# Second expert tile of an attention, expert and token-mix kernel: token list, turns and decode steps moved

## Chip, core and metric

The kernel runs on one core of a Trainium2 chip. The metric is the device time of one launch, in microseconds. Three runs of the kernel before gave 435.61, 435.96 and 431.9; the median is 435.61. One further execution was profiled.

## What is computed

Activations and expert weights are float32; the mix weights `w_theta`, `w_tok_r`, `w_tok_i` and `w_ch` come as float64 and are handed to the kernel as 64-bit words. The reference, cut to what matters:

```
attn:  B 2, H 8, S 768, D 64; each row sees its 31 neighbours and 24 block summaries
       (max of 32 keys, mean of 32 values), softmax, times values        -> x (2,768,512)
moe:   logits = x @ w_gate; a sigmoid gate may keep the expert of the token before it
       out[s] = p[e] * relu(x[s] @ w1[e]) @ w2[e]     8 experts, 512 -> 1024 -> 512
mix:   theta = x @ w_theta; zr, zi = x*cos(theta), x*sin(theta)
       y = w_tok_r @ zr + w_tok_i @ zi; u = x + y; out = u + relu(u @ w_ch)
```

## The kernel before

**Stages.** Attention runs to about 76 us of the profile. Then tokens are sorted by expert and run through expert tiles of 256 tokens: six full tiles (j = 0 to 5) and one half tile of 128 tokens, to about 248 us. The token mix takes the rest.

**A full tile.** Each tile uses one expert. Its weights come in eight pieces of 512 KB: `w1` in pieces q = 0 to 3, `w2` in q = 4 to 7. The loop variable n counts pieces over all tiles (n = 8j + q), and every piece has two half steps, so h = 2q + half runs from 0 to 15 in a tile. TensorE works on two float32r parts, high and low: three groups of matmuls take high by high, and high by low either way. `ff1` (half steps 0 to 7) makes the hidden layer, twelve 256-column matmuls a half step; `ff2` (8 to 15) adds six 512-column matmuls a half step into the output.

**What feeds it.** `load_piece` (SP's DMA queue) fills one of four `wraw` buffers, six pieces ahead where a buffer is free. `split_piece` makes the high part `whi` on ScalarE (L595) and the low part `wlo` on VectorE (L596), three pieces ahead of TensorE, into one of five buffers each; for the first three pieces GpSimd makes `wlo`. The hidden layer leaves PSUM as `hh` (ScalarE, L638) and `hl` (VectorE, L639), through three `psh` buffers. `gather` fetches the token rows of a tile by an indirect DMA of GpSimd's queue; `xpose` turns them on TensorE (256 columns of the model width a call) and splits them into `xh` (ScalarE, L618) and `xl` (VectorE, L619). The output leaves as `y` (ScalarE, L711) and `scatter` (GpSimd's queue).

**Token lists.** A generator `route0` makes the lists of tiles 0 and 1, `route1` the others, in small VectorE operations between small matmuls. Its yields "hop" mark where TensorE is needed. The last part of `route0` is a matmul into `psi` (L484), the index arithmetic (`index_pair`) and the updates of `rem` and `hib`. `HOPS` says in which half steps of tile 0 `route1` goes on: 2, 4, 6 and 9.

**Decoding.** The twelve mix weights needed first (four `t`, 512 columns; eight `w`, 768 columns) are loaded as 64-bit words and decoded between the half steps. One weight is four calls of `step(bg2)`, which this document names A to D:

```
A  ScalarE: dg and dl from the raw words (L772, L773)
B  VectorE: three bit operations on dg (L775 to L777)
C  ScalarE: high part from dg (L780)
D  VectorE: low part (L782); then the load of the weight after the next
```

The very first call only issues two loads. `dg` has one buffer, so A of the next weight comes after D. `DEC[j]` holds the half steps of tile j behind which a call stands.

**Order.** No planner moves anything: each engine takes its instructions strictly in the order in which the loop writes them. In a half step that is: loads, list work, split (first half only), matmuls with what empties PSUM, gather, scatter, turn, and last the decode call.

Of the kernel before, what the change touches and what calls it, by code (L numbers as in the profile page):

```python
# [88 lines left out]
def tile_attn_moe_mix(ctx: ExitStack, tc: tile.TileContext, qT, kT, vp, gw, w1, w2, wth, wtok, wch, cst, msk, out):  # L89
# [288 lines left out]
    def prob(b, m):  # L378
        L = lg[b][:, :, 0:8]
        ex = small([128, 6, 8], "ex")  # L380
        V.tensor_tensor(ex, L, m.unsqueeze(2).to_broadcast([128, 6, 8]), op=ALU.subtract)
        A.activation(ex, ex, AF.Exp)
        s = small([128, 6], "s")
        V.tensor_reduce(s, ex, axis=AX.X, op=ALU.add)
        V.tensor_scalar(s, s, 1.0e-9, None, op0=ALU.add)
        V.reciprocal(s, s)
        V.tensor_tensor(ex, ex, oh[b][:, 0:6, :], op=ALU.mult)
        se = small([128, 6], "se")
        V.tensor_reduce(se, ex, axis=AX.X, op=ALU.add)
        V.tensor_tensor(pe[:, 6 * b:6 * b + 6], se, s, op=ALU.mult)  # L390
# [208 lines left out]
    def gather(j):  # L599
        xgs[j] = []  # L600
        for r in range(1 if j == HT else 2):
            c = 2 * j + r if j < HT else NPX + 2 + j
            t = xg_p.tile([128, DM], F32, name="xg", tag="xg")
            G.indirect_dma_start(out=t, out_offset=None, in_=xd[0:S, :] if j < 2 else xd,  # L604
                                 in_offset=bass.IndirectOffsetOnAxis(ap=ixg[:, c:c + 1], axis=0))
            xgs[j].append(t)

    def xpose(j, c2):
        if c2 == 0:
            xts[j] = (xt_p.tile([128, 4, TS], F32R, name="xh", tag="xh"), xt_p.tile([128, 4, TS], F32R, name="xl", tag="xl"))  # L610
        xh, xl = xts[j]
        ps = psM.tile([128, 2, TS], F32, name="psx2", tag="m")
        for cc in range(2):
            for r in range(2):
                c = 2 * c2 + cc
                T.transpose(ps[:, cc, 128 * r:128 * r + 128], xgs[j][r][:, 128 * c:128 * c + 128], idn)
        s = slice(2 * c2, 2 * c2 + 2)
        A.copy(xh[:, s, :], ps)  # L618
        V.tensor_tensor(xl[:, s, :], ps, xh[:, s, :].bitcast(F32), op=ALU.subtract)  # L619

    def ff1(j, q, mm):
        hi, lo = spl[j, q]
        hw = hi.rearrange("p (c f) -> p c f", c=4)
        lw = lo.rearrange("p (c f) -> p c f", c=4)
        xh, xl = xts[j]
        if mm == 0:
            hs[j, q] = psH.tile([128, 2, TS], F32, name="psh", tag="h")
        ps = hs[j, q]
        fs = slice(128 * mm, 128 * mm + 128)
        n = 0  # L630
        for a, x in ((hw, xh), (hw, xl), (lw, xh)):
            for c in range(4):
                T.matmul(ps[:, mm, :], a[:, c, fs], x[:, c, :], start=n == 0, stop=n == 11)  # L633
                n += 1
        if mm == 1:
            hh = h_p.tile([128, 2, TS], F32R, name="hh", tag="hh")
            hl = h_p.tile([128, 2, TS], F32R, name="hl", tag="hl")
            A.activation(hh, ps, AF.Relu)  # L638
            V.scalar_tensor_tensor(hl, ps, 0.0, hh.bitcast(F32), op0=ALU.max, op1=ALU.subtract)  # L639
            hs[j, q] = (hh, hl)  # L640

    def xpose_half():
        xts[HT] = (xt_p.tile([128, 4, TS], F32R, name="xh", tag="xh"), xt_p.tile([128, 4, TS], F32R, name="xl", tag="xl"))
        xh, xl = [t[:, :, 0:128] for t in xts[HT]]
        ps = psM.tile([128, 4, 128], F32, name="psx4", tag="m")
        for c in range(4):
            T.transpose(ps[:, c, :], xgs[HT][0][:, 128 * c:128 * c + 128], idn)
        A.copy(xh, ps)
        V.tensor_tensor(xl, ps, xh.bitcast(F32), op=ALU.subtract)
# [42 lines left out]
    def ff2(j, q, r):  # L692
        hi, lo = spl[j, 4 + q]
        hw = hi.rearrange("p (c f) -> p c f", c=2)
        lw = lo.rearrange("p (c f) -> p c f", c=2)
        hh, hl = hs[j, q]
        if q == 0:
            yps[j, r] = psY.tile([128, DM], F32, name=f"psy{r}", tag=f"y{r}")
        ps = yps[j, r]
        ts_ = slice(128 * r, 128 * r + 128)  # L700
        n = 0
        for a, w in ((hh, hw), (hh, lw), (hl, hw)):
            for f in range(2):
                T.matmul(ps, a[:, f, ts_], w[:, f, :], start=q == 0 and n == 0, stop=q == 3 and n == 5)  # L704
                n += 1
        if q == 3:
            if j <= NL:
                y = ys_p.tile([128, DM], F32, name="y", tag="y")
            else:
                y = h_p.tile([128, 2, TS], F32R, name="hh", tag="hh").bitcast(F32).rearrange("p a b -> p (a b)")  # L710
            A.copy(y, ps)  # L711
            ysb[j, r] = y
# [36 lines left out]
    def scatter(j, r):  # L749
        c = 2 * j + r if j < HT else NPX + 2 + j  # L750
        G.indirect_dma_start(out=yd, out_offset=bass.IndirectOffsetOnAxis(ap=ixs[:, c:c + 1], axis=0),  # L751
                             in_=ysb[j, r], in_offset=None)
# [62 lines left out]
    def step(gen):  # L815
        return next(gen, "end")
# [90 lines left out]
    for k in range(NG + 8):  # L907
# [6 lines left out]
        if k < NG:  # L914
            n, g = units[k]
# [51 lines left out]
    def hop(gen):  # L967
        r = None
        while r not in ("hop", "end"):
            r = step(gen)  # L970
            if r == "experts":
                flags["ready"] = True
# [27 lines left out]
    def piece(fn, n):  # L1000
        if n < NPC:
            j, q = divmod(n, 8)
            fn(j if j <= NL else HT, q)
# [3 lines left out]
    items1 = [f"t{k}" for k in range(4)] + [f"w{i}{r}" for i in range(4) for r in range(2)]  # L1007
    bg2 = dec_run(items1, lambda: wk1)
    items2 = [f"w{i}{r}" for i in range(4, 6) for r in range(2)] + [f"c{k}" for k in range(4)]
    DEC = [(0, 12, 13, 14, 15)] + [(0, 2, 4, 6, 8, 9, 11, 12, 14)] * 5  # L1010
    nld = LD
    for n in range(8 * NL + 8):
        j, q = divmod(n, 8)
        for half in range(2):
            h = 2 * q + half
            while nld <= n + LD and (nld < 16 or flags["ready"]):
                piece(load_piece, nld)
                nld += 1
            if n == 0 and half == 1:
                while step(state["bg"]) != "end":  # L1020
                    pass
                gather(1)
            if j == 0 and h in HOPS or j == 1 and h == 2:
                hop(bg)
            if half == 0:
                if n < LSX:
                    piece(split_piece, n + LS)
                if n >= LSX - 1:
                    piece(split_piece, n + LS + 1)
            if q < 4:  # L1030
                ff1(j, q, half)
            else:
                ff2(j, q - 4, half)
            if h == (3 if j == 1 else 1) and j > 0:
                gather(j + 1 if j < NL else HT)
            if h == 3 and j > 0:
                scatter(j - 1, 1)
            if j == 1 and h in (7, 11):
                prob(h // 8, mmax[h // 8])
            if j > 0 and h in (10, 11):  # L1040
                if j < NL:
                    xpose(j + 1, half)
                elif half == 0:
                    xpose_half()
            elif j == 0 and h == 14:
                xpose(1, 0)
                xpose(1, 1)
            if h == 14:
                scatter(j, 0)
            if h in DEC[j]:  # L1050
                step(bg2)
    for q in range(8):
        n = 8 * NL + 8 + q
# [426 lines left out]
```

## Time and profile before

| what | value |
|---|---|
| median of three runs | 435.61 us |
| profiled execution, its own time | 431.91 us |
| its span | 430.1 us |
| TensorE matmul, weight load busy | 411.0 us (96%), 353.8 us (82%) |
| VectorE, ScalarE, GpSimd busy | 309.5 us (72%), 230.9 us (54%), 118.4 us (28%) |
| mean granted TensorE clock | 0.996 |
| weight pieces | 56 loads of 512 KB, median 4.9 us to landing |
| mix weights | 12 loads of 768 KB, median 6.8 us; 8 of 512 KB |

The span is from the first instruction's start to the last one's end; the profiled execution's own time is 1.81 us longer. A busy TensorE is not one at its peak, since matmuls are pipelined and their ends are modelled. Busy shares are averages over three stages with different limits.

### The profile page before, as it was taken

To read this page: it belongs to the slowest core of one execution; us is meant where nothing else is said; L and a number is where in the kernel's file an instruction comes from. 1 tells how busy PE (TensorE), PEld (TensorE's weight loads), DVE (VectorE), ACT (ScalarE), POOL (GpSimd) and SP (SyncE) were. 2 spreads that over 40 slices of the span, in tenths; PEclk is the share of its full clock that TensorE was granted. 3 is DMA by queue.
4 is the path that set the end of the run, shared out by engine and by line. 5 is a ranking of instruction groups with operands and counts; after the bars stand their busy time and mean duration, and the time that the engine had idled before them with its cause. 6 is when DMAs were issued, how large, how long until landed. Compare 5 with 4: busy or idle time off the path is not lost.

```text
span 430.1 us, 7952 instructions
## 1 busy us (share of the span) xinstructions
PE 411.0 (96%) x2917; PEld 353.8 (82%) x2917; DVE 309.5 (72%) x737; ACT 230.9 (54%) x424; POOL 118.4 (28%) x108
## 2 busy tenths in 40 slices
PE   8999998799899999999998899999999999999993
PEld 7677877688798989898987788888888788899883
DVE  7575668688897968987899578797988843622731
ACT  5873866645566757775678566564654421211300
POOL 8293732610122105040211121343334710100000
PEclk9999999999999999999999999999999999999998
DMA  8992984984787978989587362322300010100022
GB/s 289 409 391 79 255 263 148 339 307 139 262 269 238 337 244 271 334 261 328 191 299 243 128 231 83 104 74 84 112 26 8 28 40 24 50 13 27 12 75 80
DMA packets 45072, 76.31 MB, mean 177 GB/s; under 512 B 3424, under 2 KB 28256, under 8 KB 44256
## 3 DMA queue, kind: packets, MB, share of 16 engines
q1 hardware_dynamic: 42944, 68.89, 47.9%
q0 software_dynamic: 2080, 6.82, 4.2%
q8 instruction: 25, 0.41, 0.4%
q14 instruction: 23, 0.19, 0.1%
HBM read 62.85 MB, written 12.85 MB: 176 GB/s over the span
## 4 chain that ended last, share of the span: by engine, by line
PE 42%; ACT 3%; DVE 3%; DMA 1%; issue 1%; ACTq 0%
PE ya L1240 15%; PE yb L1240 8%; PE pth L1178 8%; PE psch L1265 8%; DVE wlo L596 1%; DMA wraw<-in_w_dram 1%; PE psxt L1115 1%; ACT whi L595 1%; PE psy L685 1%; PE pl L743 0%; ACT dg L772 0%; ACT dl L773 0%; DVE hl L639 0%; PE yb L1231 0%; DVE dg L776 0%
## 5 line engine op out<-in xcount | busy, mean ns | idle before, releaser
L596 DVE TENSOR_TENSOR wlo<-wraw,whi 128x1024 fp32r<-128x1024 f32 x53 | 64.4, 1219 | 14.0 <-ACT whi L595 14.0
L595 ACT CAST whi<-wraw 128x1024 fp32r<-128x1024 f32 x56 | 58.1, 1046 | 4.5 <-DMA wraw<-in_w_dram 3.3
L751 POOL DMA_INDIRECT yd<-y,ixs x13 | 17.0, 1307 | 118.9 <-ACT y L711 98.4
L250 ACT ACTIVATE neg<-neg,mn 128x120 f32<-128x120 f32 x96 | 30.2, 385 | 22.1 <-DVE mn L248 21.4
L633 PE MATMUL psh<-xl,whi 128*128 128x256 f32 x192 | 31.2, 284 | 2.0 <-DVE xl L619 1.9
L1208 POOL TENSOR_TENSOR r<-r,x 128x512 f32<-128x512 f32 x10 | 13.0, 1304 | 69.9 <-ACT r L1203 69.9
L633 PE MATMUL psh<-xh,whi 128*128 128x256 f32 x192 | 31.4, 285 | 0.6 <-DVE hl L639 0.6
L633 PE MATMUL psh<-xh,wlo 128*128 128x256 f32 x192 | 30.8, 283 | 0.0
L248 DVE CUSTOM_DVE_ANT_0 neg<-sps,mk 128x120 f32<-128x120 f32 x96 | 21.7, 278 | 12.5 <-PE tps L257 5.8
L704 PE MATMUL psy<-whi,hh 128*128 128x512 f32 x96 | 30.7, 401 | 0.0
L704 PE MATMUL psy<-wlo,hh 128*128 128x512 f32 x96 | 29.8, 392 | 0.0
L704 PE MATMUL psy<-whi,hl 128*128 128x512 f32 x96 | 29.8, 392 | 0.0
L633 PEld LDWEIGHTS psh<-xl,whi 128*128 128x128 f32 x192 | 26.5, 191 | 2.4 <-DVE xl L619 2.4
L633 PEld LDWEIGHTS psh<-xh,whi 128*128 128x128 f32 x192 | 26.6, 191 | 1.6 <-DVE hl L639 0.8
L242 PEld LDWEIGHTS sps<-ka,qb 128*128 128x128 f32 x192 | 23.7, 195 | 4.7 <-DVE mn L248 1.7
L242 PE MATMUL sps<-ka,qb 128*128 128x120 f32 x192 | 27.1, 286 | 0.2 <-ACT qb L214 0.2
L633 PEld LDWEIGHTS psh<-xh,wlo 128*128 128x128 f32 x192 | 26.5, 192 | 0.0
L772 ACT ACTIVATE dg<-raw 128x768 f32<-128x768 f32 (+1 forms) x20 | 16.3, 817 | 18.7 <-issue 3.7
L1271 DVE SCALAR_TENSOR_TENSOR o<-psch,xTr 128x512 f32<-128x512 f32 (+1 forms) x8 | 4.4, 552 | 28.7 <-PE psch L1265 28.7
L638 ACT ACTIVATE hh<-psh 128x512 fp32r<-128x512 f32 x24 | 14.3, 595 | 14.9 <-PE psh L633 14.8
L604 POOL DMA_INDIRECT xg<-xd,ixg x13 | 15.5, 1195 | 21.5 <-DVE ip L413 10.5
L704 PEld LDWEIGHTS psy<-whi,hl 128*128 128x128 f32 x96 | 18.0, 188 | 4.0
(462 smaller groups left out, 1151.3 us busy)
## 6 DMA issues: line engine op xcount, KB each, us to landing
wraw<-in_w_dram SPq DMA_DIRECT2D x56, 512.0 KB, 4.9
raw<-in_wtok_dram SPq DMA_DIRECT2D x12, 768.0 KB, 6.8
vall<-in_v_dram SPq DMA_DIRECT2D x6, 1040.0 KB, 9.0
kc<-in_k_dram SPq DMA_DIRECT2D x8, 400.0 KB, 6.0
qf<-in_q_dram SPq DMA_DIRECT2D x8, 384.0 KB, 6.7
xd<-xs SPq DMA_DIRECT2D x12, 256.0 KB, 5.4
yd<-zro SPq DMA_DIRECT2D x6, 512.0 KB, 6.4
x<-yd SPq DMA_DIRECT2D x12, 256.0 KB, 2.7
```

What stands on the lines that cost most here:

```text
L242: T.matmul(sps[:, c, :], qb[n % 2][:, t, :], ka[n][:, t, :], start=True, stop=True)
L248: V.tensor_tensor_reduce(out=neg[:, c, :], in0=sps[:, c, :], in1=mk[:, v, :], scale=-0.125, scalar=3.0e38, op0=ALU.add, op1=ALU.min, accum ...
L250: A.activation(neg[:, c, :], neg[:, c, :], AF.Exp, bias=mn[:, c:c + 1], scale=-1.0)
L595: A.copy(hi, r)
L596: (G if j == 0 and q < 3 else V).tensor_tensor(lo, r, hi.bitcast(F32), op=ALU.subtract)
L633: T.matmul(ps[:, mm, :], a[:, c, fs], x[:, c, :], start=n == 0, stop=n == 11)
L704: T.matmul(ps, a[:, f, ts_], w[:, f, :], start=q == 0 and n == 0, stop=q == 3 and n == 5)
L751: G.indirect_dma_start(out=yd, out_offset=bass.IndirectOffsetOnAxis(ap=ixs[:, c:c + 1], axis=0), in_=ysb[j, r], in_offset=None)
L772: A.activation(g, hw.bitcast(F32), AF.Copy, scale=2.0 ** -112)
L1178: T.matmul(pt[:, cs_], a[:, c, :], wthp[c][wi][:, cs_], start=n == 0, stop=n == 11)
L1240: T.matmul(ps, a[:, ms], w[:, t], start=part == 0 and ii == 0 and n == 0, stop=ii == 5 and n == 5 and (part == 0 or m % 2 == 1))
L1265: T.matmul(ps, wchp[c][wi][:, ms], x[:, c, t], start=n == 0, stop=n == 11)
```

## The change

The end of `route0` and the gather of tile 1's tokens move from half step 1 to half step 3 of tile 0, behind the part of `route1` that stands at half step 2. The two calls of `xpose` for tile 1, both behind half step 14 before, stand behind half steps 12 and 13. In tile 0 the decode calls at half steps 12 to 15 go; tiles 1 to 4 have one more each, at half step 5. The number of calls over all tiles stays 50, and tile 5 begins with the same call as before.

```diff
-    DEC = [(0, 12, 13, 14, 15)] + [(0, 2, 4, 6, 8, 9, 11, 12, 14)] * 5
+    DEC = [(0,)] + [(0, 2, 4, 5, 6, 8, 9, 11, 12, 14)] * 4 + [(0, 2, 4, 6, 8, 9, 11, 12, 14)]
@@
-            if n == 0 and half == 1:
+            if n == 1 and half == 1:
                 while step(state["bg"]) != "end":
                     pass
                 gather(1)
@@
-            elif j == 0 and h == 14:
-                xpose(1, 0)
-                xpose(1, 1)
+            elif j == 0 and h in (12, 13):
+                xpose(1, half)
```

## Rows read from the trace of the kernel before

**Rows 1.** PE timeline, tile 0: start, us, operation, count, idle time before and its releaser

```profile
86.93 0.30 PE L484 MATMUL psi<-rh,loh 128*128 128x2 f16 x6 [2.19 <-DVE rh L480]
...
88.60 0.33 PE L322 MATMUL psl<-idn,lt 96*128 96x96 f32 x2
...
94.78 0.38 PE L355 MATMUL bps<-idn,kt 6*128 6x6 f32 x2
```

**Rows 2.** PE timeline, start of tile 1

```profile
110.30 0.62 PE L633 MATMUL psh<-xh,whi 128*128 128x256 f32 x4
112.79 1.10 PE L633 MATMUL psh<-xl,whi 128*128 128x256 f32 x4 [1.87 <-DVE xl L619]
```

**Rows 3.** Windows of two tiles: length, busy time (instructions) by engine, clock, DMA

```profile
136.56:159.94 23.38, 23.38 (x153) 21.30 (x152) 18.81 (x23) 15.58 (x22) 3.96 (x4) 1.00 0.88 308
...
206.71:230.20 23.49, 22.91 (x148) 20.76 (x147) 21.02 (x24) 17.58 (x23) 4.75 (x3) 1.00 0.70 245
```

**Rows 4.** DVE timeline: low parts of the first pieces of tiles 2 and 5

```profile
130.74 1.22 DVE L596 TENSOR_TENSOR wlo<-wraw,whi 128x1024 fp32r<-128x1024 f32 x1
...
204.16 1.23 DVE L596 TENSOR_TENSOR wlo<-wraw,whi 128x1024 fp32r<-128x1024 f32 x1 [2.72 <-ACT whi L595]
```

**Rows 5.** Waits of ACT from 136 to 206 us: total, times, longest

```profile
ACT hh L638 <- PE psh L633: 0.7, 1, 0.7
```

**Rows 6.** Chain that ended last, in order of time: start, us, what

```profile
210.86 0.96 ACT y L711 x2
...
234.69 5.47 DMA wraw<-in_w_dram
```

**Rows 7.** DVE timeline, tile 0 and the start of tile 1

```profile
86.78 0.41 DVE L318 COPY lt<-psg 96x256 f32<-96x256 f32 x1
...
93.32 0.40 DVE L352 TENSOR_TENSOR_SCAN kt<-zro,kps 6x128 f32<-6x128 f32 x1
...
106.35 0.48 DVE L561 TENSOR_TENSOR e<-eh,cs 128x312 f16<-128x312 f32 x1
...
109.03 0.42 DVE L775 TENSOR_SCALAR db<-dg 128x512 int32<-128x512 int32 x1
...
112.06 1.28 DVE L619 TENSOR_TENSOR xl<-psx,xh 128x512 fp32r<-128x512 f32 x2
```

**Rows 8.** DVE timeline, a stretch of tile 3 without idle time between its rows

```profile
174.06 0.55 DVE L775 TENSOR_SCALAR db<-dg 128x768 int32<-128x768 int32 x1
...
176.52 0.68 DVE L639 SCALAR_TENSOR_TENSOR hl<-psh,hh 128x512 fp32r<-128x512 f32 x1
177.12 1.22 DVE L596 TENSOR_TENSOR wlo<-wraw,whi 128x1024 fp32r<-128x1024 f32 x1
178.25 0.95 DVE L782 TENSOR_TENSOR w10l<-dg,w10h 128x768 fp32r<-128x768 f32 x1
179.13 1.22 DVE L596 TENSOR_TENSOR wlo<-wraw,whi 128x1024 fp32r<-128x1024 f32 x1
```

**Rows 9.** ACT timeline, the same stretch

```profile
176.64 0.84 ACT L780 CAST w10h<-dg 128x768 fp32r<-128x768 f32 x1 [2.31 <-DVE dg L777]
177.38 1.04 ACT L595 CAST whi<-wraw 128x1024 fp32r<-128x1024 f32 x1
...
179.28 0.92 ACT L772 ACTIVATE dg<-raw 128x768 f32<-128x768 f32 x1
...
180.89 2.00 ACT L595 CAST whi<-wraw 128x1024 fp32r<-128x1024 f32 x2
```

**Rows 10.** ACT timeline: whi at half step 0 of tiles 3, 4, 5, and another

```profile
162.38 1.06 ACT L595 CAST whi<-wraw 128x1024 fp32r<-128x1024 f32 x1
...
186.90 1.05 ACT L595 CAST whi<-wraw 128x1024 fp32r<-128x1024 f32 x1
...
188.34 1.04 ACT L595 CAST whi<-wraw 128x1024 fp32r<-128x1024 f32 x1
...
211.72 1.06 ACT L595 CAST whi<-wraw 128x1024 fp32r<-128x1024 f32 x1
```

## The prediction

> **What bounds the kernel now.** I read the PE timeline first, for places where TensorE stands still in the expert stage. Tile 0 has one of 2.19 us at half step 1, where the small matmul of the second list waits for VectorE [rows 1]. Tile 1 opens with one of 1.87 us, where its second group of matmuls waits for the low part of the turned tokens [rows 2]. These are what the change goes for: 4.06 us. Then the windows by tile: tile 2 is 23.38 us long with TensorE busy for all of it, so from there the stage looks bound by TensorE [rows 3].
>
> The third view says otherwise. Piece 16, the first of tile 2, has its low part ready at 130.74 + 1.22 = 131.96, and TensorE wants it at 136.56: a lead of 4.6 us. Piece 40, the first of tile 5, is ready at 205.39 and wanted at 206.71: 1.3 us [rows 3, 4]. TensorE takes 23.38 us a tile, while ScalarE begins a tile's first split 24.52 and then 24.82 us behind that of the tile before [rows 10]. Over tiles 2 to 4 ScalarE waited for a hidden layer once, for 0.7 us [rows 5]. So ScalarE and VectorE aren't held back by TensorE there; they are slower than it and live off the lead that they had at the start. In tile 5 the lead is gone: TensorE is busy for 22.91 of 23.49 us [rows 3], and the chain that ended last runs from 210.86 over ScalarE and VectorE, and near the end through a weight load of 5.47 us that had to wait for a buffer [rows 6]. Behind 248 us the mix takes its own time, which the change doesn't touch.
>
> The end is therefore set by when the supply (ScalarE and VectorE together) finishes tile 5. TensorE's two gaps lie ahead of it, and the lead pays for them.
>
> **The list, one piece later.** Half step 1 no longer waits for the list. In place of that, the next small matmul, at half step 2, needs `lt`, which VectorE writes behind the list's last operands, at 86.78 to 87.19 [rows 7]. Half step 0 ends at 86.93 - 2.19 = 84.74; half step 1 takes 1.5 us (psi and it together 88.60 - 86.93 = 1.67 [rows 1], psi some 0.16). TensorE so waits from about 86.1 to 87.25: some 1.1 us of the 2.19 stay. From there to `bps` it needs the 94.78 - 88.60 = 6.18 us of before plus the 0.16 of psi, and arrives at 93.6. `kt` is what `bps` needs; VectorE, which has no idle time before it, ends it at 93.32 + 0.40 = 93.72 as before [rows 7], since the list arithmetic only changes its place in that queue. So the gain from here on is 94.78 - 93.75 = 1.0 us, for TensorE and for the routing chain behind it. Moved with it are two gathers on GpSimd's queue, which has nothing else between them and the first scatter; they start some 3 us later and their tokens are turned 12 us after that. SP's next wait is for a `wraw` buffer and goes with VectorE. I cost these moves at nothing.
>
> **The turn in two halves, and no decoding.** After the routing chain (its last operand at 106.35 + 0.48 before [rows 7], about 105.7 now) VectorE had two splits, B of weight t0 from 109.03, another split, and `xl` at 112.06 [rows 7]. Now `xl` stands behind two splits: 105.7 + 2 x 1.13 = 108.0, two halves of 0.6, done at 109.2. TensorE, 1.0 us ahead, opens tile 1 at 109.3 and wants `xl` half a microsecond later. This gap closes. Tile 1 starts some 3.0 us earlier, and 3.6 by its end, because the first group after the gap took 1.10 us where its like takes 0.62 [rows 2].
>
> **What the moved decode calls cost.** In tile 0 the four calls cost VectorE their work and no idle time: 106.83 and two splits make 109.1, where B starts, and B of 1.85 with a split more makes 112.0, where `xl` starts [rows 7]. In tiles 1 to 4 they stand in a queue in which ScalarE and VectorE wait for each other. The price comes from a walk through both queues in the order of the code, with the pitch from start to start [rows 8, 9]: B 2.46 (174.06 to 176.52), `hl` 0.60, `wlo` 1.13, D 0.88, C 0.74, A 1.61, whi with the two `xh` 1.90. Whi with `hh` is 1.44 [rows 10], so whi is 0.95 and `hh` 0.49. Two `xl` are taken as 1.2 and two `y` as 0.95; the t weights have 512 columns and are taken at 0.7 to 0.75 of A to D. A wait occurs where ScalarE meets C (B must be done) or A (D must be done, one buffer): 2.31 us in [rows 9]. All behind it on ScalarE, next weight piece included, waits too, and VectorE then idles for that piece, 2.72 us in [rows 4].
>
> The walk of tile 3 as it is (C, D, A, B, C, D, A, B, C) gives 24.4 us; the trace 24.52 [rows 10]. Tile 3 as changed, ScalarE's starts counted from its first whi: whi 0, A 1.25, hh 2.9, whi 3.4, hh 4.35, whi 4.85, C 8.1 (B ends then), hh 8.85, whi 9.35, A 11.35 (after D), hh 13.0, whi 13.5, C 18.2 (B was 15.7 to 18.15), whi 18.95, two xh, whi 20.85, A 23.25, whi 24.9, two y, next tile 26.8. Tile 4 walked in the same way (C, D, A, B, C, D, A, B, C, D) takes 27.15. That is 26.8 + 27.15 = 53.95 us against 24.52 + 24.82 = 49.34: 4.6 us more for two calls more, and one more of the calls at which ScalarE blocks.
>
> Tiles 1 and 2, walked from tile 1's start with TensorE's new times, reach whi of tile 3 at 161.3, against 162.38 [rows 10]: 1.1 us ahead, but with two calls still owed. Then whi of tile 4 comes at 188.1 (before 186.90) and of tile 5 at 215.2 (before 211.72). There the decode state is that of before, and the last D ends 3.3 us later than it did. TensorE's 3.6 us are used up at the end of tile 3, where the first piece of tile 4 is ready only at 182.4 against a start at 180.0.
>
> **Sum.** -1.0 (routing earlier) -2.6 (B and D of t0, of 1.85 and 0.6 or so, off VectorE before tile 1, 0.1 for their wait) gives VectorE 3.6 ahead; the four calls added later cost +2.4 of the same work and +4.5 of blocking: +3.3 in all. Tile 5 and the half tile have no slack to take it in. The profiled execution would become 431.91 + 3.3 = 435.2. Its own time lies 3.7 below the median of the runs shown, so on that scale 435.61 + 3.3 = 438.9.
>
> **Bounds.** Blocking is the unknown. Lower end: it doesn't grow, because idle time of ScalarE and VectorE takes it in; then only the earlier routing counts, -1.1. Middle: each blocking call costs what it does now, (49.34 - 2 x 11.5 of splits, `hh`, `xh`, `y`) / 9 = 2.9 us, so one more in tiles 3 and 4 is +2.9 and the end +1.6. Upper end: tile 2, which the walk lets off with 0.6, pays as tiles 3 and 4 do, 2.3; the end is +5.0. I take the walk's 3.3, since it gives tile 3 of before to 0.1 us.
>
> **Rivals.**
> (1) *The supply keeps up.* The blocking was idle time anyway; TensorE's gain shrinks to that of the routing, -1.1: 434.5. For it: over the same calls the work is unchanged. Against: [rows 9] and [rows 4], where a blocked ScalarE leaves VectorE idle for more than two microseconds. Not slower than before.
> (2) *TensorE's gaps are the price.* Both vanish and nothing takes their place: -3.6, 432.0. For it: TensorE is busy for 96% of the span and for all of tile 2. Against: the lead falls from 4.6 to 1.3 us [rows 3, 4], and TensorE would have to be served 3.6 us earlier than that. [...]
> (3) *Blocking in tile 2 as well.* C right behind B, A right behind D at neighbouring half steps: if tile 2 pays 2.3 us like the two after it, the lead is gone a tile earlier and the end is +5.0: 440.6. It decides where `wlo` of piece 24 comes later than 156 us. For it: the new place, half step 5, stands directly ahead of half step 6 and so shortens the time that B or D has. Against: the t weights of tiles 1 and 2 are smaller by a third.
>
> **Numbers.** Forecast 0.60, rival (1) 0.18, rival (2) 0.07, rival (3) 0.15. Predicted 438.9. The range goes from rival (2) to a little over rival (3), 432.2 to 441.3: the runs before differ by 4 us among themselves, which no part of this sum narrows. About 1% (4.36 us) is what a measurement of this kernel can tell from no change. Rival (3) is slower by more, with a part of the forecast's upper side; none reaches 1% faster by itself, only rival (2) with a low set of runs. Faster 0.05, within 1% 0.76, slower 0.19.
>
> **What would show it.** Right: in tile 0 a wait of about 1.1 us ahead of `psl` in place of that for psi; no wait for `xl` in tile 1, which starts near 109.3; ScalarE's first whi of tiles 3, 4, 5 near 161, 188 and 215; TensorE waiting for whi or `xl` from the start of tile 4; the mix starting some 3 us later than 248. Wrong: leads that stay over 1 us through tile 4, or whi of tile 5 before 211.7; then the blocking was mis-sized, and rival (1) or (2) holds.

## Result and profile after

The changed kernel is slower by 0.57%: ratio 1.0057, 95% interval 1.0038 to 1.0076, median 436.23 us against 434.32 over 17 runs each. By the ratio that is some 2.5 us, by the difference of the medians 1.9. The predicted 438.9 lay 3.3 us over the median of the three runs shown, and lies 4.6 over that of the 17. The profiled executions differ by more, 438.17 against 431.91: the one after is the longest of its 17, and of the 17 before only two were shorter than the profiled one.

The page of the changed kernel, its span and busy times:

```profile
span 436.4 us, 7951 instructions
PE 413.8 (95%) x2917; PEld 355.3 (81%) x2917; DVE 310.6 (71%) x737; ACT 231.2 (53%) x424; POOL 119.0 (27%) x108
```

Its PE timeline (start, us, operation, count, idle time before and its releaser) at the places of [rows 1, 2], and where tile 4 opens:

```profile
84.45 0.74 PE L633 MATMUL psh<-xh,whi 128*128 128x256 f32 x4
...
88.67 0.39 PE L322 MATMUL psl<-idn,lt 96*128 96x96 f32 x2 [1.08 <-DVE lt L318]
...
95.15 0.38 PE L355 MATMUL bps<-idn,kt 6*128 6x6 f32 x2
...
110.66 0.63 PE L633 MATMUL psh<-xh,whi 128*128 128x256 f32 x4
111.13 0.64 PE L633 MATMUL psh<-xl,whi 128*128 128x256 f32 x4
...
167.24 0.74 PE L633 MATMUL psh<-xh,whi 128*128 128x256 f32 x4 [0.64 <-DVE hl L639]
...
183.58 0.99 PE L633 MATMUL psh<-xh,whi 128*128 128x256 f32 x4 [1.33 <-ACT xh L618]
184.96 1.10 PE L633 MATMUL psh<-xl,whi 128*128 128x256 f32 x4 [0.38 <-DVE xl L619]
```

The wait for psi of 2.19 us has become one for `lt` of 1.08. Tile 1 opens without a wait: its second group comes 26.7 us behind the start of tile 0 (84.45), against 29.7 for that in [rows 2]. And TensorE, which waited for nothing from there to tile 5 before, now waits in tile 3 for a low part of the hidden layer (0.64 us, at 167.24) and stands still where tile 4 opens.

ScalarE's timeline of the changed kernel shows where its pieces come late. The whi at 162.91, 189.97 and 217.42 answer to those at 162.38, 186.90 and 211.72 in [rows 10], the waits to [rows 9]:

```profile
162.91 1.06 ACT L595 CAST whi<-wraw 128x1024 fp32r<-128x1024 f32 x1
...
171.15 0.83 ACT L780 CAST w01h<-dg 128x768 fp32r<-128x768 f32 x1 [2.32 <-DVE dg L777]
...
174.39 0.93 ACT L772 ACTIVATE dg<-raw 128x768 f32<-128x768 f32 x1 [0.97 <-ACT whi L595]
...
176.47 1.04 ACT L595 CAST whi<-wraw 128x1024 fp32r<-128x1024 f32 x1
181.26 0.83 ACT L780 CAST w10h<-dg 128x768 fp32r<-128x768 f32 x1 [3.75 <-DVE dg L777]
182.00 1.04 ACT L595 CAST whi<-wraw 128x1024 fp32r<-128x1024 f32 x1
...
186.45 0.93 ACT L772 ACTIVATE dg<-raw 128x768 f32<-128x768 f32 x1 [1.49 <-issue]
...
189.97 1.06 ACT L595 CAST whi<-wraw 128x1024 fp32r<-128x1024 f32 x1
192.86 0.83 ACT L780 CAST w11h<-dg 128x768 fp32r<-128x768 f32 x1 [1.83 <-DVE dg L777]
...
217.42 1.06 ACT L595 CAST whi<-wraw 128x1024 fp32r<-128x1024 f32 x1
```

Between 176.47 and 182.00 ScalarE makes no weight piece: it stands at C of weight w10 (w10h) for 3.75 us, since B is still on VectorE. The next whi, first piece of tile 4, comes at 182.00, and right behind it TensorE gets its `xh` at 183.58. VectorE's timeline over the same time has B, and then VectorE's own wait for the piece that ScalarE could not make:

```profile
178.69 0.55 DVE L775 TENSOR_SCALAR db<-dg 128x768 int32<-128x768 int32 x1
179.28 0.96 DVE L776 SCALAR_TENSOR_TENSOR dg<-dg,db 128x768 int32<-128x768 int32 x1
180.27 0.96 DVE L777 CUSTOM_DVE_ANT_0 dg<-dg,dl 128x1536 uint16<-128x1536 uint16 x1
183.08 1.22 DVE L596 TENSOR_TENSOR wlo<-wraw,whi 128x1024 fp32r<-128x1024 f32 x1 [1.85 <-ACT whi L595]
```

A wait of 3.75 us is nothing new by itself: ScalarE had one ahead of w00h before, in tile 2. What is new shows in the sums of the windows from the first whi of tile 3 over that of tile 4 to that of tile 5, before and then after:

```profile
sum 49.34, PE 49.34 PEld 45.18 DVE 41.75 ACT 33.78 POOL 10.56; mean PE 24.67 PEld 22.59 DVE 20.88 ACT 16.89 POOL 5.28
sum 54.54, PE 49.76 PEld 43.10 DVE 42.83 ACT 35.60 POOL 11.35; mean PE 24.88 PEld 21.55 DVE 21.42 ACT 17.80 POOL 5.68
```

The two tiles take 5.2 us more, but VectorE (DVE) is busy for only 1.1 us more and ScalarE (ACT) for 1.8: for most of the time added, each of the two is idle.

Below, "stage" is the time from the first `psh` matmul to the first `psxt` matmul, read from the PE timelines. It is 165.1 us in the profile before and 254.55 - 84.45 = 170.1 after. Attention ahead of it ended at other times in each profile (its code is the same), so stages are compared, and ratios of runs for the whole.

### The profile page after: what moved, and what is told of

Its sections match the earlier page's. It is cut to its first block, busy times and chain, and to the rows that moved or that the text cites. A ratio compares the mean times of both kernels' runs of the same rounds, so it can differ in the third digit from the quotient of the medians.

```text
span 436.4 us, 7951 instructions
## 1 busy us (share of the span) xinstructions
PE 413.8 (95%) x2917; PEld 355.3 (81%) x2917; DVE 310.6 (71%) x737; ACT 231.2 (53%) x424; POOL 119.0 (27%) x108
## 5 line engine op out<-in xcount | busy, mean ns | idle before, releaser
L633 PE MATMUL psh<-xh,whi 128*128 128x256 f32 x192 | 32.3, 289 | 4.4 <-DVE hl L639 2.7
L242 PE MATMUL sps<-ka,qb 128*128 128x120 f32 x192 | 28.2, 294 | 1.3 <-DVE ka L234 0.7
L242 PEld LDWEIGHTS sps<-ka,qb 128*128 128x128 f32 x192 | 24.8, 203 | 5.6 <-DVE ks L230 1.7
L639 DVE SCALAR_TENSOR_TENSOR hl<-psh,hh 128x512 fp32r<-128x512 f32 x24 | 16.5, 687 | 6.8 <-ACT hh L638 6.5
```

What stands on the lines that cost most here:

```text
L242: T.matmul(sps[:, c, :], qb[n % 2][:, t, :], ka[n][:, t, :], start=True, stop=True)
```

## Experiments

All ratios are to the kernel before on the same chip, with 95% intervals.

**The two halves of the change.** First the moves without the new decode list:

```diff
-    DEC = [(0,)] + [(0, 2, 4, 5, 6, ...)] * 4 + [...]     (changed kernel)
+    DEC = [(0, 12, 13, 14, 15)] + [(0, 2, 4, 6, 8, 9, 11, 12, 14)] * 5
```

> Changed kernel with the decode calls of before (five in tile 0, nine in each other tile); only the list and the turn are moved. Blocking theory (the added calls in tiles 1 to 4 make ScalarE wait for VectorE, the moves themselves are a small gain): 2 us under before, ratio 0.993 to 1.000, ScalarE's first whi of tile 5 up to 2 us earlier than before's 211.7 (set against the same start of tile 0). Rival A (the moved list or turn is what costs): as slow as the changed kernel, ratio 1.004 to 1.008. Rival B (TensorE's gaps are the price): 3 to 4 us under before, 0.991.

Measured: 0.9896 (0.9854 to 0.9938), 429.51 us, 4.5 us under before by the ratio; stage 162.9. ScalarE's first whi of tile 5 comes 126.2 us behind tile 0's start, against 128.7. The gain is over the 2 us expected, and of the size that rival B gave. Then the other half, the new list on the kernel before:

```diff
-    DEC = [(0, 12, 13, 14, 15)] + [(0, 2, 4, 6, 8, 9, 11, 12, 14)] * 5
+    DEC = [(0,)] + [(0, 2, 4, 5, 6, 8, 9, 11, 12, 14)] * 4 + [(0, 2, 4, 6, 8, 9, 11, 12, 14)]
```

> Kernel before with the new list of decode calls alone (one in tile 0, ten in tiles 1 to 4, half step 5 added). Blocking theory: slower than the changed kernel, 4 to 6 us over before, ratio 1.009 to 1.014; the delay arises in tiles 3 and 4. Rival A (the moves cost): no slower than before, 0.995 to 1.001.

Measured: 1.0100 (1.0064 to 1.0135), 438.26 us; stage 172.7. ScalarE takes 27.1 and 27.4 us from the first whi of tile 3 to that of 4 and of 5, against 24.5 and 24.8: the delay arises there, as expected. So the moves are a gain and the list is the loss; rival A falls on both. Rival B is right on the size of the moves, but as what decides the whole change it falls too, since the changed kernel has neither gap and is slower. The moves alone gain 4.5 us where the stage shows 2.2, which the section on reasons takes up.

**Number or place of the calls.** The tenth call of tiles 1 to 4 stands behind another half step; number and work are those of the changed kernel:

```diff
-    [(0, 2, 4, 5, 6, 8, 9, 11, 12, 14)] * 4
+    [(0, 2, 4, 6, 8, 9, 11, 12, 14, 15)] * 4
```

> Changed kernel with the tenth decode call of tiles 1 to 4 behind half step 15 instead of 5; the number of calls, and the work, are those of the changed kernel. Blocking theory: the order of A to D against the splits decides, not the number; walked in the same way as in the prediction, ScalarE blocks less, TensorE is not caught up in tiles 3 to 5, and the kernel is 4 to 6 us under before, ratio 0.986 to 0.991. Rival C (the added work itself costs, wherever it stands): as the changed kernel, 1.004 to 1.008.

Measured: 0.9817 (0.9784 to 0.9850), 426.73 us; stage 159.0. That is a larger gain than expected. The same edit with 7 in place of 15:

> Changed kernel with the tenth decode call of tiles 1 to 4 behind half step 7 instead of 5. Blocking theory, by the same walk: blocks worse than half step 5, 3 us over the changed kernel and 6 to 7 over before, ratio 1.012 to 1.017. Rival C (work alone): as the changed kernel, 1.004 to 1.008.

Measured: 1.0105 (1.0071 to 1.0139), 439.13 us; stage 172.8: slower than before as expected, by 4.6 us and not 6 to 7. The same with 10:

> Changed kernel with the tenth call of tiles 1 to 4 behind half step 10 instead of 5. Blocking theory, by the same walk: as good as half step 15, TensorE not caught up through tile 5, 6 us off the stage of before, ratio 0.979 to 0.986. Rival D (what helps at half step 15 is that the call stands at the end of a tile, where little is queued): near the changed kernel, 1.000 or more.

Measured: 0.9837 (0.9808 to 0.9865), 426.47 us; stage 160.7. One call, moved within the tile, changes the kernel by 12 us. The supply moves with it: ScalarE's first whi of tile 5 comes 136.4 us behind tile 0's start with the call behind 7, 133.0 behind 5, 123.9 behind 10 and 122.9 behind 15. Work by amount (rival C) is out, and so is the end of the tile as what helps (rival D). The waits of VectorE from 136 to 206 us, changed kernel first (total, times, longest):

```profile
DVE wlo L596 <- ACT whi L595: 9.6, 11, 2.7
```

and with the call behind half step 15:

```profile
DVE wlo L596 <- ACT whi L595: 4.3, 8, 1.8
```

The kernel before has 10.6 us of this wait over the same stretch, so its total tells a supply that is late from one that is early only together with what TensorE does. With the call behind 15 the trace shows no wait of TensorE from 100 to 230 us, and ScalarE waits for TensorE again in tiles 2 to 4, as a supply does that keeps ahead. Waits of ACT from 137 to 208 us:

```profile
ACT xh L618 <- PE psx L616: 2.9, 3, 1.2
...
ACT hh L638 <- PE psh L633: 2.2, 3, 1.3
...
ACT w10h L780 <- DVE dg L777: 0.6, 1, 0.6
```

The wait ahead of w10h is 0.6 us where it was 3.75.

**The one buffer of dg.** Two buffers, first in the changed kernel:

```diff
-            return dtp.tile([128, 768], dt, name=name, tag=name)[:, 0:n]
+            return dtp.tile([128, 768], dt, name=name, tag=name, bufs=2 if name == "dg" else 1)[:, 0:n]
```

> Changed kernel with two buffers of dg (3 KB a partition more), so that call A of the next weight no longer waits for call D of the last; the order of all calls stays. Blocking theory: ScalarE's waits ahead of dg go, those ahead of C stay, and the walk makes the expert stage some 5 us shorter than in the kernel before: ratio 0.983 to 0.990. Rival C (the added work costs, wherever it stands): as the changed kernel, 1.004 to 1.008.

Measured: 0.9859 (0.9826 to 0.9893), 427.25 us; stage 160.6. In the kernel before:

> Kernel before with two buffers of dg. Blocking theory: the supply of tiles 3 to 5 is quicker here too, but TensorE's two gaps in tiles 0 and 1 stay, so TensorE is the bound sooner: 1.5 to 3 us under before, ratio 0.990 to 0.998, less than what two buffers give the changed kernel. Rival C: no change.

Measured: 0.9914 (0.9884 to 0.9944), 430.0 us; stage 162.5. With the work and its order kept, taking away one cause of ScalarE's waits turns the change from a loss of 0.6% into a gain of 1.4%, and gains 0.9% without it. ScalarE's waits show which one. The changed kernel from 137 to 208 us:

```profile
ACT w10h L780 <- DVE dg L777: 3.7, 1, 3.7
ACT dg L772 <- issue: 3.7, 2, 2.2
...
ACT dg L772 <- ACT whi L595: 2.6, 4, 1.0
...
ACT dg L772 <- DVE t3l L782: 1.9, 1, 1.9
```

and with two buffers from 134 to 204 us:

```profile
ACT w10h L780 <- DVE dg L777: 3.7, 1, 3.7
...
ACT dg L772 <- DMA raw<-in_wtok_dram: 0.7, 1, 0.7
```

The waits ahead of A (dg) fall from 8.2 to 0.7 us, while the one ahead of C of w10 stays at 3.7. So that wait, which stood ahead of the late piece above, does not by itself make the change a loss; it takes the waits at A beside it. Both edits on the changed kernel, call behind 15 and two buffers:

> Changed kernel with the tenth call behind half step 15 and two buffers of dg: both of the edits that shortened the stage. Blocking theory: with the call at 15 TensorE already waits for nothing in tiles 1 to 5, so two buffers find little left: 0 to 1 us under the kernel with the call at 15 alone, ratio to before 0.979 to 0.984. If blocking still held that kernel back: 0.975 or less.

Measured: 0.9819 (0.9790 to 0.9849), 425.69 us; stage 159.1. Nothing is left that the second buffer could be seen to take: this version and the call behind 15 alone can't be told from each other, and both beat the kernel before and the changed one.

**The two moves one by one.** On the kernel before, first the list with the gather, then the turn (each as in the diff of the change):

> Kernel before with the list's end and the gather one piece later, nothing else. Blocking theory: only the part of the wait that becomes free, 0.5 to 1 us under before in the expert stage, which starts with the wait for lt of 1.1 us in place of 2.2; ratio 0.994 to 1.000. If the list were most of the gain of both moves: 0.990.

Measured: 0.9956 (0.9935 to 0.9978), some 1.9 us; stage 165.4, with a wait of 1.09 us for `lt`.

> Kernel before with the turn of tile 1 in two halves behind half steps 12 and 13, nothing else; the decode calls behind 12 to 15 stay. Blocking theory: tile 1 opens without its wait of 1.9 us and ScalarE and VectorE are some 1 us earlier from there: stage 1 to 1.5 us shorter than before, ratio 0.993 to 0.999. If the turn were of no use without the decode calls gone: 1.000.

Measured: 0.9945 (0.9921 to 0.9969), some 2.4 us; stage 165.1, without a wait for `xl`. Together they make 4.3 us, near the 4.5 of both. Each is more than its expectation's middle, but neither stage is shorter than the 165.1 of the first profile before, as was expected: each of the two still has one gap, and behind it the granted clock fell (0.64 from 112 to 116 us with the list alone, 0.57 from 86 to 90 with the turn alone), which the next runs take up.

**Both kernels once more**, unchanged:

> Kernel before, unchanged, profiled once more: how much of a difference between two profiled executions comes from run to run, and in which stage. If the expert stage (first psh matmul to first psxt matmul, 165.1 us before) comes out within 0.5 us, stages can be compared between single profiles and the rest is in attention.

Measured: 434.43 us, stage 168.0, not within 0.5 us: 2.9 us more than in the first profile, with the same two gaps ahead of tile 5. What differs is the granted clock behind the two gaps. Windows of the first profile before, then of the second (length, busy time and instructions of PE, PEld, DVE, ACT, POOL, then granted clock, DMA):

```profile
88.00:92.00 4.00, 4.00 (x36) 3.90 (x35) 3.73 (x21) 1.68 (x3) 1.91 (x2) 1.00 1.02 391
...
116.00:120.00 4.00, 4.00 (x38) 4.00 (x35) 3.42 (x11) 2.26 (x4) 2.17 (x2) 1.00 0.76 237
```

```profile
87.00:90.00 3.00, 3.00 (x16) 3.00 (x16) 2.23 (x11) 0.28 (x1) 1.24 (x2) 0.51 1.01 403
...
88.00:92.00 4.00, 4.00 (x26) 4.00 (x26) 2.78 (x18) 1.53 (x2) 1.91 (x2) 0.69 1.03 409
...
116.00:120.00 4.00, 4.00 (x37) 3.96 (x37) 1.22 (x4) 2.04 (x3) 0.00 (x0) 0.78 0.93 317
```

And the PE timeline of the second profile behind its first gap:

```profile
86.72 0.30 PE L484 MATMUL psi<-rh,loh 128*128 128x2 f16 x6 [2.18 <-DVE rh L480]
86.88 1.03 PE L633 MATMUL psh<-xh,whi 128*128 128x256 f32 x4
87.71 1.05 PE L633 MATMUL psh<-xl,whi 128*128 128x256 f32 x4
...
90.59 0.64 PE L633 MATMUL psh<-xl,whi 128*128 128x256 f32 x4
```

Four matmuls take 1.03 us directly behind the gap, in which TensorE stood still for 2.18 us, and 0.64 us from 90.59 on, 3.7 us after the first of them; the granted clock was 0.51 from 87 to 90. The second group of tile 1 comes 31.2 us behind tile 0's start, against 29.7, and ScalarE's first whi of tile 3 at 82.2, against 79.3. So 1.5 us of the 2.9 are there by tile 1 and all of them by tile 3, in the supply too.

> Changed kernel, unchanged, profiled once more: if the expert stage is again near 170.1 us, the added 5 us are the change's; if it comes out nearer 167.5, the first profile was a long one and the 2.5 us of the medians are the true size.

Measured: 436.51 us, stage 170.9. The change's stage is near 170.5 both times; it is the kernel before that varies more. The changed kernel's second profile lost the clock as well, but behind the wait where tile 4 opens, and the first did not. Their windows behind that wait, first profile first:

```profile
186.00:189.00 3.00, 3.00 (x27) 3.00 (x26) 1.50 (x2) 2.55 (x3) 0.00 (x0) 1.00 0.61 157
```

```profile
184.00:186.00 2.00, 2.00 (x11) 2.00 (x11) 0.98 (x1) 2.00 (x3) 0.00 (x0) 0.50 0.32 124
```

There it cost little: ScalarE's first whi of tile 5 comes at 133.0 and 133.1 us, and the stages differ by 0.8.

## Why the prediction was right, and where its sizes were off

**What bounds.** Right. The supply bounds the end: its order moved the kernel by 12 us (call behind 7 against 15 or 10) with TensorE's work unchanged. That the lead pays for TensorE's two gaps holds in part only: at the same clock the moves alone shorten the stage by 2.2 us, and in the profile of the kernel before in which the clock fell behind the gaps (0.51 from 87 to 90 us) the stage is 2.9 us longer.

**The list and the turn.** Right in place and size: a wait of 1.08 us for `lt` (1.1 predicted, though the terms given, 84.74 + 1.5 up to 87.25, make 1.0), `bps` 10.7 us behind tile 0's start in place of 11.7 (1.0 predicted), tile 1 opening 26.2 us behind tile 0 (109.3 - 83.05 = 26.2), no wait for `xl`.

**The decode calls.** Right in kind, short in size. ScalarE's first whi of tiles 3, 4 and 5, counted from tile 0's start, was predicted at 78.2, 105.0 and 132.2 us; it came at 78.5, 105.5 and 133.0. The kernel before has 79.3, 103.9 and 128.7, so the supply is 4.3 us late at tile 5 where the sum said 3.5 for whi and 3.3 for the last D. The half tile added 0.7 more, to 5.0 at the mix, where some 3 was forecast.

**The sum.** Two of its sizes were off, and that 3.3 came near the 2.5 measured is in part luck, since they offset each other. The first is the list. In profiles in which the clock stayed up (1.00 in the windows of the stage), the stage is 165.1 before, 162.9 with the moves alone and 170.1 with both: the moves gain 2.2 us, where the sum has 1.0 for the routing, and the list costs 7.2, where the sum has -2.6 + 2.4 + 4.5 = 4.3. Net that is 5.0 in place of 3.3.

The second is what TensorE's gaps cost the kernel before. The prediction priced them by their length in one profile, in which the clock stayed at 1.00, and noted that this execution lay 3.7 us under the median without asking why. The second profile of before gives a reason: behind both gaps there the granted clock was low (0.51 from 87 to 90 us, 0.57 from 114 to 118), and the stage is 2.9 us longer. Against that profile the change costs 170.1 or 170.9 - 168.0 = 2.1 to 2.9 us, and the ratio says 2.5. The moves are worth 4.5 us by the ratio and 2.2 or 5.1 by the stages, against the first or the second profile, for the same reason.

The second profile is the common case. Its mean granted clock is 0.987, that of the first 0.996. Of 49 further executions of the kernel before, 26 lie at 0.990 or less (median 434.5 us), 15 at 0.991 or 0.992 (432.9) and 8 at 0.994 or more (432.5). No run sets the clock, so that it makes this difference is read from where in the profiles the time is lost, not from an experiment.

**Rivals.** (1), the supply keeps up, and (2), TensorE's gaps are the price: out for this kernel, since the supply was caught at tile 4. With the call behind half step 15 or 10 the supply does keep up, and the gain of 8.0 or 7.1 us is more than either rival gave, since the supply there is quicker than in the kernel before. The moves that go for the gaps of (2) were a real gain of 4.5 us by themselves; with the decode calls moved as well, ScalarE and VectorE stood idle for 3.4 and 4.1 us longer in tiles 3 and 4 (windows above), and the gain was lost. (3), blocking in tile 2 too: its condition did not come, though its size of 5.0 us did in the stage. VectorE starts `wlo` of piece 24 before 156 us, 70.9 us behind tile 0's start (72.5 before), and whi of tile 3 was 0.2 us off the walk:

```profile
155.36 1.22 DVE L596 TENSOR_TENSOR wlo<-wraw,whi 128x1024 fp32r<-128x1024 f32 x1 [2.73 <-ACT whi L595]
```

**The level.** The predicted 438.9 added the 3.3 us to a median of three runs; 14 further runs took that median from 435.61 to 434.32. Of the 2.7 us by which 438.9 lies over the measured 436.23, this is 1.3.

## What to carry to other kernels

Where two in-order engines hand work to each other in pieces, the place of a piece in the order can count for more than its size (12 us here for one call, moved within the tile): walk both queues with start-to-start pitches before adding a step, and look for the step at which the consumer stands directly behind its producer. A lead that shrinks from tile to tile (4.6 to 1.3 us here) can show that the busy engine isn't the bound before a single wait does. Don't price an idle gap of TensorE from one profile without checking the granted clock behind it (1.00 in one profile of the kernel before, 0.51 in the other), and ask why one profile lies apart from the median.

## What the hardware showed

Behind a gap of TensorE of about 2 us the granted clock fell in some profiles and not in others. The second profile of the kernel before, where it fell behind both gaps, has 1.5 us more than the first by the start of tile 1 and 2.9 us more of stage. In the profiles here nine gaps of 1.87 to 2.19 us occur in tiles 0 and 1; behind six of them the granted clock in the lowest window of 4 us (78 to 82 us and on) was 0.57 to 0.70, behind three it stayed at 1.00, two of these in the profile on which the prediction rests. By an estimate from these windows, in which each of the six is short of 1.7 us at full clock, it was near 0.50 for some 3.5 us. Of the waits of 1.04 to 1.09 us for `lt`, in nine profiles, none was followed by a lower clock there (1.00 from 82 to 94 us). Where tile 4 opens, four profiles have a wait for `xh`: behind 2.04 us (call behind 7: 0.50 from 186 to 190 us) and behind 1.34 us (the new decode list alone: 0.58 from 186 to 190; the changed kernel's second profile: 0.50 from 184 to 186) the clock fell, behind 1.33 us (the changed kernel's first: 1.00 from 186 to 189) it did not. Where tile 0 starts behind attention, 81.3 to 85.1 us with the same code, differs from profile to profile by more than the change is worth; the cause of that stays open.
